# Projections as 64-row halves between the score products of a two-tower attention kernel

## The chip, the cores and the metric

The kernel runs on one core of one Trainium2 chip. The metric is the device time of one execution in microseconds (us); lower is better. The engines are PE (TensorE matmul, with its weight loads shown as PEld), DVE (VectorE), ACT (ScalarE), POOL (GpSimd) and SP (SyncE, which here only issues DMAs).

## What is computed

Two attention blocks share the input x (2048 tokens, 640 features), each with its own weights; each has 32 heads of 20 features. A sigmoid gate mixes the two results.

```python
qkv = (x @ wqkv).reshape(B, S, 3, H, Dh)          # S=2048, H=32, Dh=20, for A and for B
scores = einsum("bhqd,bhkd->bhqk", q, k) * Dh ** -0.5
p = softmax(scores, axis=-1)
o = einsum("bhqk,bhkd->bhqd", p, v)
y = o.transpose(0, 2, 1, 3).reshape(B, S, D) @ wo
out = g * y_A + (1 - g) * y_B                      # g = sigmoid((x * gate_w).sum(-1))
```

## The kernel before

The 64 heads are taken in 16 groups of four. For each group and each block of 512 queries the kernel makes eight steps of 256 keys, 512 steps in all; the number of a step is `G`. PE works in tiles of 64 rows by 32 columns in nearly all of a step: side 0 is rows 0 to 63 of the array, side 1 rows 64 to 127, and what one side does runs beside what the other does. The order of PE's work in a step is written out by hand in the table `STEP` (line 55), by these letters, with the side as the digit:

- `e0`, `e1`: the score product of one head, 128 keys by 512 queries (`scores`, line 704; four matmuls at line 167 in the four column tiles of a side). ACT then takes the exponential of the bank (line 714).
- `m0`, `m1`: a second score product, queries by keys, that only serves to find the maximum of a later step's rows (`max_mm`, line 638; the same line 167). DVE reduces the bank (line 665), or ACT takes a Relu (line 658) and DVE finishes (line 662). A step has eight `e` and about eight `m`, of which one goes to ACT.
- `V0`, `V1`: half of the values product of the step before (`values`, line 724, matmuls at line 730), accumulated in the side's own accumulator `acc0` or `acc1`; four per side and step. One is float32 and two passes long.
- `X`: a turn for one block of the linear layers, by `slot` (line 1229): a part of a chunk of Q/K projection (`project_chunk`), a V projection of 128 tokens (`project_v`) or a part of an output row block (`out_tiles`). Each block is 6 to 15 matmuls of 128 rows by 128 columns in the helper `mms` (line 442), all into one bank, followed by one copy (ACT lines 469, 608, 800, 803, DVE line 806).

Products go to PSUM banks. Two of the eight are the accumulators; six (`bank0` to `bank5`, shown as bank_90 to bank_95) are shared by `e`, `m` and blocks. `take` (line 139) gives a product the bank that by the planner's clock comes free first; `give` returns it with the time at which its reader will be done. The choice is made when the program is built, so on the chip a product waits for just that bank's last reader, and PE takes its instructions in order.

Of a chunk (512 tokens) three or four parts were made, each a block of its own with its own bank and copy (`CUTS`, `APARTS`, `RPARTS`); `behind` decides whether a step has none, one or two blocks. In the last steps, where no maxima are left, `LATE` stands for `STEP`.

Of the kernel before, what the change touches and what calls it, by code (L numbers as in the profile page):

```python
# [19 lines left out]
P = 128  # L20
# [6 lines left out]
GH = 4  # L27
# [11 lines left out]
CUTS = {3: (0, 176, 344, 512), 4: (0, 128, 256, 384, 512), 5: (0, 104, 208, 312, 416, 512), 6: (0, 88, 176, 264, 344, 432, 512)}  # L39
APARTS = {2: 4, 3: 4, 4: 4, 5: 4, 6: 4}  # L40
RPARTS = {1: 4}
# [10 lines left out]
OFINE = (16, 16, 6, 16)  # L52


STEP = ("e1 V0 m1 e1 V0 m1 e0 V1 m0 e0 V1 m0 m1 V0 e1 m1 V0 e1 m0 V1 e0 m0 V1 e0",
        "e1 V0 m1 e1 V0 m1 e0 V1 m0 e0 V1 m0 X m1 V0 e1 m1 V0 e1 m0 V1 e0 m0 V1 e0",
        "e1 V0 m1 e1 V0 m1 e0 V1 m0 e0 V1 m0 X m1 V0 e1 m1 V0 e1 m0 V1 e0 m0 V1 e0 X")
LATE = "e1 V0 e1 V0 e0 V1 e0 V1 X e1 V0 e1 V0 e0 V1 e0 V1"
# [14 lines left out]
def kernel(  # L73
# [80 lines left out]
    def tick_score(j, i):  # L154

        clock["pe"] = max(clock["pe"], rows_free[j], free_at[i])
        rows_free[j] = clock["pe"] + T_SCORE
        clock["done"] = max(clock["done"], clock["pe"] + T_READY)
        return clock["done"]

# [8 lines left out]
    def tick_values(j, ready):  # L169

        clock["pe"] = max(clock["pe"], rows_free[j], ready)
        rows_free[j] = clock["pe"] + T_VALUES
        clock["done"] = max(clock["done"], rows_free[j] + T_READY - T_SCORE)

# [259 lines left out]
    def mms(i, out_ap, pairs, cost):  # L434

        if now[0] >= 0:
            tick_block(len(pairs) * cost * T_SCORE, free_at[i])
        for k, (a, b) in enumerate(pairs):
            if now[0] < 0:
                tick_block(cost * T_SCORE, free_at[i])  # L440
                streamed[0] += cost * T_SCORE
            nc.tensor.matmul(out_ap, a, b, start=(k == 0), stop=(k == len(pairs) - 1))  # L442
            if now[0] < 0:
                yield True

# [5 lines left out]
    def project_chunk(w, hi, lo, ch, parts=None):  # L451
# [9 lines left out]
        if now[0] >= 0:  # L461
            f = work.tile([P, QB], F32, name="fs")
            for k in range(len(parts) - 1):
                if k:
                    yield
                m = slice(parts[k], parts[k + 1])
                i, pt = take()
                yield from mms(i, pt[:, m], pairs(slice(t0 + m.start, t0 + m.stop)), (m.stop - m.start) / QB)
                nc.scalar.activation(f[:, m], pt[:, m], AF.Copy, scale=QKS)  # L469
                give(i, spend("act", 0.25, clock["done"]))  # L470
            nc.gpsimd.tensor_copy(hi, f)  # L471
            nc.gpsimd.tensor_tensor(lo, f, hi, op=OP.subtract)
        else:
            i, pt = take()
            yield from mms(i, pt, pairs(slice(t0, t0 + QB)), 1)
# [42 lines left out]
    def project_r(i, ch):  # L518
        n = slice(ch * QB, (ch + 1) * QB)
        yield from project_chunk(blk["r", i], rk[i][:, 0, n], rk[i][:, 1, n], ch, CUTS[RPARTS.get(i, 3)])  # L520
# [25 lines left out]
    def project_a(g, ch):  # L546
# [4 lines left out]
        yield from project_chunk(blk["a", g], hl[:, 0, n], hl[:, 1, n], ch, CUTS[APARTS.get(g, 3)])  # L551
# [45 lines left out]
    def project_v(gg, j):  # L597

        wh, wl = blk["v", gg]
        w = 161 if gg == 0 else 160  # L600
        for u in range(2):
            if u and now[0] >= 0:
                yield
            n = slice((j + u) * P, (j + u + 1) * P)
            i, pt = take()
            yield from mms(i, pt[:, :w], [(a[:, c, n], b[:, c, :w]) for c in range(NC) for a, b in
                                          ((xh, wh), (xh, wl), (xl, wh))], 0.33)
            nc.scalar.activation(V[gg % 2][:, j + u, :, 0:DH], pt[:, :160].rearrange("p (h d) -> p h d", h=2 * GH),
# [115 lines left out]
    def values(G, kk, side, part):  # L724
# [4 lines left out]
        for h in range(GH):  # L729
# [3 lines left out]
            if side and part:  # L733
                ptiles.pop((G, kk, h))
# [33 lines left out]
    def out_tiles(job, t, state):  # L768
# [15 lines left out]
        cuts = (0, 216, 432, 640) if t >= OFINE[jobs.index(job)] else (0, 320, 640)  # L784

        def products():
            wh, wl = wo_parts[z]
            for k, end in zip(cuts, cuts[1:]):
                if k:
# [4 lines left out]
                yield from mms(i, pt[:, :width], [(o[:p, a, c - c0], w[:p, c, n])  # L794
                                                  for c in range(c0, c1) for p in (P if c < full else 48,)
                                                  for a, w in ((0, wh), (0, wl), (1, wh))], width / QB)
                f = f_o[z][:, t:t + 1]
# [21 lines left out]
        soon(state["due"], len(cuts) - 1, products())  # L819

    def take_acc(g, qb):
# [3 lines left out]
        nc.scalar.activation(total, accs[0], AF.Copy)  # L825
# [4 lines left out]
        nc.vector.tensor_tensor(total, accs[1], total, op=OP.add)  # L830
# [80 lines left out]
    def last_tiles(qb, o):  # L911
# [3 lines left out]
        for t in range(4):  # L915
            c = slice(t * P, (t + 1) * P)
            f = f_o[1][:, 4 * qb + t:4 * qb + t + 1]
            for half in range(2):
# [3 lines left out]
                tick_block(0.4, free_at[i])  # L922
                for k, (a, w) in enumerate(((0, wh), (0, wl), (1, wh))):
                    nc.tensor.matmul(pt[:, :320], o[:, a, c], w[:, n], start=(k == 0), stop=(k == 2))  # L924
# [234 lines left out]
    for g in range(2 * NG):  # L1159
        b = g * step  # L1160
        n = g + 1
        if n < 2 * NG:
            parts = APARTS.get(n, 3)
            fill += [((-8, 15)[g] if g < 2 else b + AFROM, b + ADUE + ADUES * ch if g else 4 + 3 * ch, parts, project_a(n, ch))
# [4 lines left out]
            if i < 4:  # L1169
# [5 lines left out]
                if g % 4 == 2:  # L1175
                    tasks(b + 6, 3, weights_r(i))
                    parts = RPARTS.get(i, 3)
                    fill += [(b + 12, b + 26 + 6 * ch if i == 1 else b + 22 + 4 * ch, parts, project_r(i, ch)) for ch in range(4)]
            gg = g // 2 + 1
            if gg < NG and g % 2 == 0:  # L1180
# [5 lines left out]
                fill += [(max(b + 2, 12), b + 2 * step - 4 + j // 2, 2, project_v(gg, j)) for j in range(0, NT, 2)]  # L1186
# [21 lines left out]
    def out_tasks(G):  # L1208
# [8 lines left out]
        if last and all(4 * last[0][0] + t in summed for t in range(4)):  # L1217
            soon(now[0] + 6, 4, last_tiles(*last.pop(0)))

    def behind(G):  # L1220

        n = sum(f[0] for f in current)
        for f in sorted((f for f in fill if f[0] <= G), key=lambda f: f[1]):
# [133 lines left out]
```

## Time and profile before

| what | value |
|---|---|
| median of 3 runs | 2828.87 us (2828.64 to 2833.61) |
| the profiled execution | 2828.82 us |
| its span, first to last instruction | 2827.0 us |
| busy share PE, PEld, DVE, ACT, POOL | 98%, 56%, 87%, 89%, 25% |
| granted clock of PE, mean | 0.999 |
| first and last exponential begin at | 100.8 and 2807.3 us |

A row of the page's groups names the line, the engine, the operation, what is written and read with the shapes, the count, then the busy time in us and the mean duration of one in ns, and after the second bar the idle time of the engine before these instructions with what ended most of it. A row of the timeline begins with the start in us and the time until the last of the merged instructions ends. The durations of PE's matmuls are modelled, so their starts are read and not their ends.

### The profile page before, as it was taken

What the parts mean: (1) busy time and instruction counts of PE and PEld (TensorE: products, weight loads), DVE (VectorE), ACT (ScalarE), POOL (GpSimd) and SP (SyncE); (2) the same over time, 40 slices, a digit from 0 to 9 for tenths busy, and PEclk for the clock granted to TensorE, in tenths of its full rate; (3) what the DMA queues carried; (4) which work ended last, traced back from release to release, by engine and by line L of the source; (5) the groups of instructions that cost most, each with busy time, mean ns of one, the idle gap of its engine ahead of it and who ended that gap; (6) DMA issues with size and microseconds to landing.
All of it is one profiled execution on the core that took longest, in us unless ns stands there. A gap on an engine that the chain in (4) does not pass through costs nothing.

```text
span 2827.0 us, 163418 instructions
## 1 busy us (share of the span) xinstructions
PE 2784.2 (98%) x72102; PEld 1593.8 (56%) x72102; DVE 2460.6 (87%) x4777; ACT 2530.0 (89%) x5211; POOL 697.8 (25%) x1009
## 2 busy tenths in 40 slices
PE   9999999999999999999999999999999999999998
PEld 4555555555555555665555555555566555555444
DVE  8789898898899989888888898989988888999982
ACT  4999999999999999999999889989999888999887
POOL 6132222222123422212122122223342202101111
PEclk9999999999999999999999999999999999999999
DMA  4021102010120212102021230211201112132112
GB/s 142 17 58 25 33 18 44 9 35 18 24 56 20 66 45 53 36 13 62 21 54 49 68 87 23 69 51 47 66 20 42 36 47 64 34 80 63 46 50 76
DMA packets 175809, 132.05 MB, mean 47 GB/s; under 512 B 103672, under 2 KB 145456, under 8 KB 175096
## 3 DMA queue, kind: packets, MB, share of 16 engines
q1 hardware_dynamic: 172552, 120.31, 16.7%
q8 instruction: 563, 9.22, 1.3%
q0 software_dynamic: 1600, 0.96, 0.2%
q14 instruction: 150, 1.23, 0.1%
q10 hardware_dynamic: 944, 0.33, 0.0%
HBM read 55.53 MB, written 31.86 MB: 31 GB/s over the span
## 4 chain that ended last, share of the span: by engine, by line
PE 85%; ACT 8%; DVE 3%; issue 2%; DMA 1%; POOL 1%; ACTq 0%; SPq 0%; POOLq 0%; DVEq 0%
PE bank L167 43%; PE acc L730 20%; PE bank L442 20%; ACT pt L714 7%; DVE mpart L665 2%; PE bank L164 1%; DMA ws<-in_A_wqkv_dram 0%; PE bank L924 0%; PE acc L442 0%; DMA xs<-in_A_x_dram 0%; DMA kt<-mrow 0%; ACT rl L658 0%; DVE rl L662 0%; DVE y_out L806 0%; ACT ob L825 0%
## 5 line engine op out<-in xcount | busy, mean ns | idle before, releaser
L714 ACT ACTIVATE pt<-bank 128x512 f32<-128x512 f32 x4096 | 2172.5, 633 | 190.2 <-PE bank L167 145.4
L665 DVE TENSOR_REDUCE mpart<-bank 128x1 f32<-128x512 f32 x2944 | 1875.0, 681 | 255.6 <-PE bank L167 166.2
L730 PE MATMUL acc<-pt,v 64*21 64x256 f32 x32768 | 2068.8, 380 | 12.1 <-DVE ob L830 10.5
L167 PE MATMUL bank<-qt,kt 64*32 64x512 f16 x16384 | 1572.2, 380 | 3.4 <-ACT pt L714 0.7
L167 PE MATMUL bank<-kt,qt 60*32 60x512 f16 x13824 | 1364.2, 380 | 2.5 <-ACT pt L714 0.6
L167 PEld LDWEIGHTS <-kt 64*32 64x32 f16 x16384 | 603.5, 91 | 460.2 <-issue 327.4
L167 PEld LDWEIGHTS <-qt 60*32 60x32 f16 x15872 | 553.2, 90 | 413.6 <-issue 223.2
L730 PEld LDWEIGHTS acc<-pt,v 64*21 64x21 f32 x32768 | 686.9, 96 | 134.2 <-DVE ob L830 27.9
L662 DVE CUSTOM_DVE_ANT_0 rl<-bank,rl 128x512 f32<-128x512 f32 x568 | 384.4, 680 | 16.3 <-PE bank L167 10.0
L658 ACT ACTIVATE rl<-bank 128x512 f32<-128x512 f32 x569 | 375.0, 664 | 5.1 <-PE bank L164 4.7
L442 PE MATMUL bank<-xx,wbh 128*128 128x168 f16 (+3 forms) x2450 | 276.8, 234 | 5.1
L442 PE MATMUL bank<-xx,wbl 128*128 128x168 f16 (+3 forms) x1225 | 253.3, 233 | 0.0
L442 PEld LDWEIGHTS <-wbh 128*128 128x128 f16 x2480 | 197.3, 98 | 70.1 <-issue 60.2
L841 POOL TENSOR_TENSOR ot<-ot,sq 128x512 f32<-128x512 f32 x63 | 66.0, 1048 | 609.8 <-DVE sq L838 609.8
L167 PE MATMUL bank<-kd,qt 60*32 60x512 f16 x2048 | 203.9, 380 | 0.0
L471 POOL CAST cq<-fs 128x512 f16<-128x512 f32 x60 | 36.6, 610 | 516.2 <-ACT fs L469 516.2
L442 PE MATMUL bank<-woh,o_in 128*128 128x320 f16 (+3 forms) x700 | 157.4, 289 | 2.5
L442 PEld LDWEIGHTS <-xx 128*128 128x128 f16 x1920 | 133.3, 97 | 41.1 <-issue 37.2
L442 PE MATMUL bank<-wvh,xx 128*128 128x160 f16 (+1 forms) x1250 | 153.3, 234 | 2.4
L442 PE MATMUL bank<-wvl,xx 128*128 128x160 f16 (+1 forms) x625 | 134.4, 232 | 0.0
L442 PEld LDWEIGHTS <-o_in 128*128 128x128 f16 (+1 forms) x1050 | 90.1, 97 | 66.8 <-issue 44.8
L442 PEld LDWEIGHTS <-wbl 128*128 128x128 f16 x1240 | 121.0, 98 | 4.7 <-issue 1.3
(184 smaller groups left out, 1444.0 us busy)
## 6 DMA issues: line engine op xcount, KB each, us to landing
y_scr<-y_out SPq DMA_DIRECT2D x48, 320.0 KB
y_out<-y_scr SPq DMA_DIRECT2D x32, 320.0 KB
kt<-cq SPq DMA_DIRECT2D x120, 80.0 KB
o_scr<-on SPq DMA_DIRECT2D x240, 40.0 KB
o_in<-o_scr SPq DMA_DIRECT2D x64, 96.0 KB
kt<-cq SPq DMA_DIRECT2D x136, 40.0 KB
wstage<-in_B_wqkv_dram SPq DMA_DIRECT2D x13, 400.0 KB
xs<-in_A_x_dram SPq DMA_DIRECT2D x8, 640.0 KB
```

The lines of the kernel that those rows point to most:

```text
L164: nc.tensor.matmul(pt, stationary, moving, start=True, stop=True)
L167: nc.tensor.matmul(pt[c:c + 32], stationary[:, c:c + 32], moving, start=True, stop=True)
L442: nc.tensor.matmul(out_ap, a, b, start=(k == 0), stop=(k == len(pairs) - 1))
L471: nc.gpsimd.tensor_copy(hi, f)
L658: nc.scalar.activation(relus[u, j], pt, AF.Relu)
L662: nc.vector.tensor_tensor_reduce(rl, pt, rl, 1.0, LOW, OP.add, OP.max, m)
L665: nc.vector.tensor_reduce(m, pt, axis=AX.X, op=OP.max)
L714: nc.scalar.activation(pt, et, AF.Exp, scale=factor(g // 4))
L730: nc.tensor.matmul(accs[side][32 * h:32 * h + VW, c], V[(g // 2) % 2][r, kt, (g % 2) * GH + h, :], ptiles[G, kk, h][r, c], start=(kt == 0 ...
L841: nc.gpsimd.tensor_tensor(t3, t3, sq.unsqueeze(2).to_broadcast([P, 16, 32]), op=OP.mult)
```

## The change

Inside the 512 steps the linear layers no longer run as blocks of 128-row matmuls. `mms` hands its list of products to `weave_job`, which cuts each product at row 64 into a half for side 0 and a half for side 1. `halves_of` issues the halves between the scores: each as four matmuls of 64 rows by 32 columns, at the places `x0` and `x1` of the step's order. All halves of a job accumulate into one bank, which is taken when the job begins and held until the copy after its last half. The halves of one side stand in one cluster and those of the other side in a second cluster, so that the two sides do not write the bank at the same time; `recent` sees to it that a bank of a score has come round between the clusters. A place takes one half of 512 columns, or three of the V projection's 160 columns (cost 0.33), or one or two of an output's 320 columns (cost 0.625).

The chunk is made whole: one job of 15 products of 512 columns, three steps of five halves per side, with one copy. The V projection makes two token blocks in one job of 30 products, with one copy of 320 columns. Of all outputs two parts are made. `begin` starts a job at the beginning of a step and picks the order of the step: 0 (no job), `FEW` (five places per side) or `MANY` (six, where that ends the job).

```diff
-STEP = (...
-        "e1 V0 m1 e1 V0 m1 e0 V1 m0 e0 V1 m0 X m1 V0 e1 m1 V0 e1 m0 V1 e0 m0 V1 e0",
...
+FEW, MANY = 5, 6
+STEP = {0: "e1 V1 V1 m1 V0 e1 m1 e0 m0 V1 e0 m0 e0 V0 V0 m1 m0 V1 e0 m0 e1 V0 m1 e1",
+        FEW: "e1 x0 x0 V1 x0 x0 V1 x0 m1 V0 e1 m1 e0 m0 V1 e0 m0 x1 e0 x1 x1 V0 x1 x1 V0 m1 m0 V1 e0 m0 e1 V0 m1 e1",
...
+    def weave_job(i, entries, cost):
+        w = {"bank": i, "cost": cost, "n": 0, "credit": [0.0, 0.0], "q": ([], [])}
+        for a, b, cols in entries:
+            for side in range(2):
+                r = slice(64 * side, min(64 * side + 64, a.shape[0]))
+                if r.start < r.stop:
+                    w["q"][side].append((a[r], b[r], cols))
+        w["all"] = len(w["q"][0]) + len(w["q"][1])
+        recent["side"] = None
+        weave.append(w)
+        while weave:
+            yield
...
+    def halves_of(side, most=1.0):
+        w = weave[0]
+        q = w["q"][side]
+        if not q or recent["side"] == 1 - side and not recent["known"]:
+            return
+        recent.update(side=side, banks=set(), known=False)
+        w["credit"][side] += most
+        while q and w["credit"][side] >= w["cost"] - 1e-6:
+            w["credit"][side] -= w["cost"]
+            a, b, cols = q.pop(0)
+            w["n"] += 1
+            for c in range(0, P, 32):
+                nc.tensor.matmul(banks[w["bank"]][c:c + 32, cols], a[:, c:c + 32], b, start=(w["n"] == 1),
+                                 stop=(w["n"] == w["all"]), skip_group_check=True)
...
-                i, pt = take()
-                yield from mms(i, pt[:, m], pairs(slice(t0 + m.start, t0 + m.stop)), (m.stop - m.start) / QB)
-                nc.scalar.activation(f[:, m], pt[:, m], AF.Copy, scale=QKS)
-                give(i, spend("act", 0.25, clock["done"]))
+            i, pt = take()
+            yield from mms(i, slice(0, QB), pairs(slice(t0, t0 + QB)), 1)
+            nc.scalar.activation(f, banks[i], AF.Copy, scale=QKS)
+            give(i, spend("act", T_EXP, clock["done"]))
...
+        if now[0] >= 0:
+            i, pt = take()
+            yield from weave_job(i, [(a[:, c, slice((j + u) * P, (j + u + 1) * P)], b[:, c, :w], slice(u * w, u * w + w))
+                                     for u in range(2) for c in range(NC) for a, b in ((xh, wh), (xh, wl), (xl, wh))], 0.33)
+            nc.scalar.activation(V[gg % 2][:, j:j + 2, :, 0:DH],
+                                 pt[:, :2 * w].rearrange("p (t h d) -> p t h d", t=2, h=2 * GH), AF.Copy, scale=QKS)
```

How many instructions the built programs hold: the four-matmul score groups and the values products are as many as before (8064 groups, 16384 matmuls). The linear layers inside and before the steps go from 6786 matmuls of 128 rows (lines 442 and 924) to 492 of these and 29208 of 64 rows. ACT's chunk copies go from 240 to 72 and its V copies inside the steps from 112 to 56. SP's queue and POOL's casts hold the same work. Of the 512 steps, 462 now have halves (before, 490 had a block).

Three places of PE's order, all in or at the end of step 210, show the new places. In the rows below, `kt,qt` or `kd,qt` after the bank is an `m`, `qt,kt` an `e`, `acc_88` and `acc_89` are the accumulators of side 0 and side 1, and every product of scores or halves is four rows of which one is shown. First, the middle of step 210 before: an `m0`, the block of 15 matmuls in its bank 93, then `m1`, `V0` and `e1`.

```order
L730 MATMUL acc_89<-pt,v_87 21x256 x4
...
L167 MATMUL bank_94<-kt_83,qt_81 32x512
...
L442 MATMUL bank_93<-xx,wbh 128x168
...
L442 MATMUL bank_93<-xx,wbl 128x168
...
L167 MATMUL bank_90<-kt_83,qt_81 32x512
...
L730 MATMUL acc_88<-pt,v_87 21x256 x4
...
L167 MATMUL bank_91<-qt_80,kt_82 32x512
```

This block is gone. Second, the beginning of step 210 in the changed program, from its first `e1` (bank 93) to its first `m1` (bank 91): the job's bank is 95, and after the first `V1` come two more halves, the second `V1` and a fifth half, whose rows read like those shown.

```order
L162 MATMUL bank_93<-qt_80,kt_82 32x512
...
L498 MATMUL bank_95<-xx,wbl 32x512
...
L498 MATMUL bank_95<-xx,wbh 32x512
L795 MATMUL acc_89<-pt,v_87 21x256 x4
...
L162 MATMUL bank_91<-kt_83,qt_81 32x512
```

Between the first `e1` and the first `m1` there now stand a cluster on side 0 and two values products on side 1, where one `V0` stood. Third, what follows this `m1` in the changed program, up to the `e0` within the second cluster; the `kd,qt` is the `m0` that ACT reads.

```order
L795 MATMUL acc_88<-pt,v_87 21x256 x4
...
L162 MATMUL bank_92<-qt_80,kt_82 32x512
...
L162 MATMUL bank_90<-kt_83,qt_81 32x512
...
L162 MATMUL bank_94<-qt_80,kt_82 32x512
...
L162 MATMUL bank_93<-kd_85,qt_81 32x512
...
L795 MATMUL acc_89<-pt,v_87 21x256 x4
...
L162 MATMUL bank_91<-qt_80,kt_82 32x512
...
L162 MATMUL bank_92<-kt_83,qt_81 32x512
...
L498 MATMUL bank_95<-xx,wbl 32x512
...
L162 MATMUL bank_94<-qt_80,kt_82 32x512
```

With the `m1` ahead of these rows, eight score products now follow one another with two values products among them, and they use five banks, since bank 95 is the job's: the sixth takes the first's bank (91), the seventh the second's (92), the eighth the fourth's (94). After the second cluster, which ends with two `V0`, the order goes on in the same way with `m1` (90), `m0` (93), `e0` (92), `m0` (91), `e1` (94), `m1` (90), `e1` (92) and, as the first of step 211, `e1` (93).

More of the change, by code (lines that the diff above doesn't have):

```diff
@@ L432, in weights_r, with mms @@
         return load, split
-    def mms(i, out_ap, pairs, cost):
+    weave = []
+    def weave_job(i, entries, cost):
[10 more added lines that the diff above has]
+            yield
+    def mms(i, n, pairs, cost):
+        if 0 <= now[0] < STEPS:
+            yield from weave_job(i, [(a, b, n) for a, b in pairs], cost)
+            return
         if now[0] >= 0:
@@ L1185 @@
                 at(max(b - 1, 10), split)
[L1186 removed]
+                fill += [(max(b + 2, 12), b + 2 * step - 14 + j, 20, project_v(gg, j)) for j in range(0, NT, 2)]
     early = weights_v(NG - 1)
@@ L1288 @@
             product()
-            slot(G)
+            for side in (0, 1):
+                fence()
+                begin(G)
+                for _ in range(4):
+                    slot(G, side)
         some = next_maxima(G, 4)
-        blocks = 0 if not current and not any(f[0] <= G for f in fill) else 2 if behind(G) else 1
+        order = (STEP if maxima or some else LATE[G % 2])[begin(G)]
         count = {}
-        for what in (STEP[blocks] if maxima or some else LATE + " X" * (blocks == 2)).split():
+        for what in order.split():
             k = count[what] = count.get(what, 0) + 1
```

149 lines of the change are left out of this document (91 added, 58 removed).

## Prediction

> **What bounds the kernel now.** I read the page's busy shares and its chain first, then the groups, and last the timeline of one step, engine by engine. The page:
>
> ```profile
> PE 2784.2 (98%) x72102; PEld 1593.8 (56%) x72102; DVE 2460.6 (87%) x4777; ACT 2530.0 (89%) x5211; POOL 697.8 (25%) x1009
> ...
> PE bank L167 43%; PE acc L730 20%; PE bank L442 20%; ACT pt L714 7%; DVE mpart L665 2%; PE bank L164 1%; DMA ws<-in_A_wqkv_dram 0%; PE bank L924 0%; PE acc L442 0%; DMA xs<-in_A_x_dram 0%; DMA kt<-mrow 0%; ACT rl L658 0%; DVE rl L662 0%; DVE y_out L806 0%; ACT ob L825 0%
> ...
> L714 ACT ACTIVATE pt<-bank 128x512 f32<-128x512 f32 x4096 | 2172.5, 633 | 190.2 <-PE bank L167 145.4
> L665 DVE TENSOR_REDUCE mpart<-bank 128x1 f32<-128x512 f32 x2944 | 1875.0, 681 | 255.6 <-PE bank L167 166.2
> ...
> L167 PE MATMUL bank<-qt,kt 64*32 64x512 f16 x16384 | 1572.2, 380 | 3.4 <-ACT pt L714 0.7
> ```
>
> The chain lies on PE for 85%, ACT and DVE are busy for nearly nine tenths, and where these two idle they wait for PE's scores. None of the three is full. What ties them shows only in one step. These are PE's rows from one block to the next (starts are what counts):
>
> ```profile
> 1001.18 0.32 PE L442 MATMUL bank<-xx,wbh 128*128 128x168 f16 x2
> ...
> 1002.21 0.24 PE L442 MATMUL bank<-xx,wbl 128*128 128x168 f16 x1
> 1002.38 0.40 PE L167 MATMUL bank<-kt,qt 60*32 60x512 f16 x4
> 1002.39 0.41 PE L730 MATMUL acc<-pt,v 64*21 64x256 f32 x4
> 1002.60 0.39 PE L167 MATMUL bank<-qt,kt 64*32 64x512 f16 x4
> ...
> 1002.82 0.39 PE L167 MATMUL bank<-kt,qt 60*32 60x512 f16 x4
> ...
> 1003.92 0.78 PE L167 MATMUL bank<-qt,kt 64*32 64x512 f16 x8
> 1004.32 0.41 PE L730 MATMUL acc<-pt,v 64*21 64x256 f32 x4
> ...
> 1004.80 0.40 PE L167 MATMUL bank<-qt,kt 64*32 64x512 f16 x4
> ...
> 1005.29 0.40 PE L167 MATMUL bank<-qt,kt 64*32 64x512 f16 x4
> ...
> 1005.78 0.40 PE L167 MATMUL bank<-qt,kt 64*32 64x512 f16 x4
> ...
> 1006.04 0.37 PE L167 MATMUL bank<-kt,qt 60*32 60x512 f16 x1
> ...
> 1006.37 0.33 PE L442 MATMUL bank<-xx,wbh 128*128 128x176 f16 x2
> ```
>
> After the block a score product begins every 0.22 us (1002.38, 1002.60, 1002.82): that is what one product takes of a side, and a values product, two passes, takes two such slots, 0.43. From 1004.80 on the pairs come 0.49 apart (1004.80, 1005.29, 1005.78): PE waits. For what, ACT's and DVE's rows tell:
>
> ```profile
> 1002.48 0.31 ACT L469 ACTIVATE fs<-bank 128x168 f32<-128x168 f32 x1
> 1003.17 3.54 ACT L714 ACTIVATE pt<-bank 128x512 f32<-128x512 f32 x7 [0.38 <-PE bank L167]
> ```
>
> ```profile
> 1002.89 1.29 DVE L665 TENSOR_REDUCE mpart<-bank 128x1 f32<-128x512 f32 x2 [0.85 <-PE bank L167]
> ```
>
> An `e` that begins at 1002.60 is read from 1003.17: 0.57 later. An `m` of 1002.38 is read from 1002.89: 0.51 later. Seven exponentials take 3.54, one lasts 0.633, so they follow at (3.54-0.633)/6 = 0.485; two reductions take 1.29 and one 0.681, so 0.61. The third exponential thus ends at 3.17+2x0.485+0.633 = 4.77 (I leave out the thousand), and the product of 4.80 begins; the fourth ends at 5.26, and that of 5.29 begins; the fifth at 5.74, and that of 5.78 begins. In the program's order these are the users of the same banks, and the hand-over takes 0.03 to 0.04. So PE's products wait for a bank, and **a bank costs 0.57+0.633+0.04 = 1.24 us for an `e`, 0.51+0.681+0.04 = 1.23 for an `m`, plus the reader's queue.** Six banks and this turnaround set the burst of 16 products; then comes the block, in which ACT and DVE run dry (0.38 and 0.85).
>
> I check this as a rule: every product starts at the latest of its side's slot, the product ahead of it in the order, and the release of its bank. From `m1` at 0 it gives 0, 0.22, 0.44, 0.65, 0.87, 1.08, 1.30, 1.52 (PE's pace), then by releases 1.94, 2.16, 2.42, 2.64, 2.90, 3.12, 3.37, 3.64 and the block at 3.95. The rows say 4.32-2.38 = 1.94 for the `V0` right behind the ninth, 2.42 and 2.91 for the eleventh and thirteenth, and 3.99 for the block. The rule holds within 1% here. All steps:
>
> ```profile
> L714 ACT ACTIVATE pt<-bank x4096: 590/632/1006, 100.8 to 2807.3; 128x512 f32<-128x512 f32 x196
> ```
>
> (2807.3-100.8)/512 = 5.29 us, against 6.37-1.18 = 5.19 in this one, so some 0.1 us per step is other work in the readers' queues that the rule doesn't have.
>
> **The change, part by part.**
>
> *The drains around blocks.* The last matmul of the block begins at 1002.21, matmuls there follow at (1002.21-1001.18)/14 = 0.074, and the next product begins at 1002.38: 0.10 lost. Ahead of the block at 1006.37 the last score began at 1006.04 and had 0.22 to stream: 0.11 lost. Together 0.2 us for each of 490 blocks, 98 us of PE's time that goes. PE's own need hardly falls, though: in a step with 5+5 halves a side has 8 slots of scores, 4 values products and 5 halves, 8x0.217+4x0.433+5x0.217 = 4.55 us, and before it had 3.47 and a block of 1.1 with its drains, 4.77.
>
> *The copies.* Rows of ACT's groups by shape: V copies, chunk copies in three sizes, and a copy of 320 columns:
>
> ```profile
> L608 ACT ACTIVATE v<-bank 128x160 f32<-128x160 f32 x125 | 38.5, 308 | 13.1 <-PE bank L442 12.8
> ...
> L469 ACT ACTIVATE fs<-bank 128x128 f32<-128x128 f32 x96 | 31.7, 330 | 3.3 <-PE bank L442 1.2
> L469 ACT ACTIVATE fs<-bank 128x168 f32<-128x168 f32 x96 | 30.7, 320 | 11.8 <-PE bank L442 11.6
> L800 ACT ACTIVATE y_out<-bank,f_o 128x320 f32<-128x320 f32 x32 | 16.9, 527 | 9.2 <-PE bank L442 7.5
> L469 ACT ACTIVATE fs<-bank 128x176 f32<-128x176 f32 x48 | 15.3, 318 | 9.3 <-PE bank L442 6.0 <-issue 1.9
> ```
>
> 240 chunk copies cost 77.7 us of ACT and become 72 of the size of an exponential, 72x0.633 = 46; 112 V copies at 0.308 = 34 become 56 at 0.527 = 30. ACT loses some 36 us of work. Off the path: the copies stand where ACT waits for scores (the 1002.48 row lies ahead of its 0.38 of idling), so I take 0; on the path it would be -36.
>
> *The order and the banks: the large term.* A job keeps its bank from its first half to its copy, three steps for a chunk, so scores have five banks, where before a block held one for about 1.1 us and its copy. And the step now has two stretches without a score instead of one. I apply the same rule to step 210, whose banks the order shows, from its first `m1` at 0, the queues empty. First burst: `e1` 0.22, `m1` 0.44, `e0` 0.44, `m0` 0.66 are at PE's pace. The sixth (`e0`, bank 91) waits for the first `m1`: 1.23. The seventh (bank 92) waits for the `e1`: 0.22+1.24 = 1.46. The eighth (`e0`, bank 94) waits for the `e0` of 0.44, which stands second in ACT's queue: 0.22+0.57+0.485+0.633+0.04 = 1.95. Then come the other four halves of the second cluster, on side 1, 0.217 each, which hold back `m1`: 2.82. Second burst: `m0` 3.03, `e0` 3.25, `m0` and `e1` 3.47; `m1` in bank 90 waits for the `m1` of 2.82: 4.05; `e1` in bank 92 for the `e0` of 3.25: 4.49; the next step's `e1` for its side, 4.71 (its bank, the `m0`'s of 3.03, is free at 4.66). Then on side 1 that `e1` and two `V1`, 0.217+2x0.433 = 1.08, ahead of the next `m1`: **5.79 us**, against 3.95+15x0.074+0.10 = 5.16 by the same rule before. PE waits 0.36+0.27+0.36+0.22 = 1.21 for banks (without them it would be 4.58), and in each of the two gaps ACT and DVE idle: ACT needs 9x0.485 = 4.37 of 5.79. Behind a waiting score stand the halves and values products of both sides, since PE takes its instructions in order, so the clusters can't fill the wait.
>
> Where the planner always gave the bank that comes free first, the eighth would start at 1.84 and the step take 5.68; that is the lower end. At the upper end the 0.1 us of other work falls into each burst and delays more than itself: 6.05. I take 5.79+0.1 = 5.89, the other work of the average step before. For the 50 steps without halves the rule gives 5.1 with six banks (the two values products between the bursts stay), and the last 14, without maxima, stay as they are: 5.0 on average.
>
> *Issue.* The halves bring 22,900 more pairs of weight load and matmul. The four matmuls of a product take 0.40 from the first's start to the last's end (the row of 1002.38) where one alone takes 0.380, so they start within 0.02, and a values product on the other side starts 0.01 after them; I take issue as 0, with a rival for the other case.
>
> *Sum.* Before 512x5.29 = 2706. After 462x5.89+50x5.0 = 2971. That is +265 on the profiled execution's 2828.8 us, which is the median of the runs shown (2828.87) within 0.1: **3094 us**. The lower end, 462x5.68+250 = 2874, gives 2997; the upper, 462x6.05+250 = 3045, gives 3168.
>
> **The rivals.**
>
> *Drains alone (faster).* If scores rarely wait for a bank, the gain is PE's drains: 2829-98 = 2731. The mechanism: halves run beside `V1` and `V0`, so nothing stops while they stream, and readers are fed in two smaller portions. It decides once a step stays under (2706-250)/462 = 5.32 us, that is if the waits for banks come to under 5.32-4.58-0.1 = 0.64 us in a step instead of 1.21. For it speaks that PE is busy 98%; against it that the same rule hit the step before to 1% with a bank more. The Trainium skill, TensorEngine Tiling (Array Packing), Key Properties, says that a change of tiling mode drains the engine; the trace agrees, with 0.2 us around a block, and by that rule alone the change gains these 98 us. I give it 0.11.
>
> *Copies or nothing.* The bursts' waits are as long as the drains saved, and the step stays at 5.29: 2829, or with the copies' 36 us on the path 2793. 0.04.
>
> *Issue-bound V steps (slower still).* 112 steps would carry 15+15 halves of 160 columns: 32+32 matmuls of scores, 64 passes of values, 120 of halves, 248 pairs. The closest that the step shown has them is a score group and a pass of values, eight pairs, in 0.22 us: 27 ns. At that price 248 pairs take 6.7 us instead of 5.89: +91, 3185. Against it: there PE streams, and issue isn't what is short. The Trainium skill, TensorEngine Tiling (Array Packing), Instruction Overhead, has about 60 cycles for each matmul; no run here shows one by itself. By it, an estimate at the 2.4 GHz of its page TensorE: Matmul & The Clock Gate, 216 matmul instructions at 25 ns make 5.4 us, under the 5.89, and the rival falls. 0.05.
>
> **How the numbers follow.** Forecast 0.80, drains alone 0.11, nothing or copies 0.04, issue 0.05. A measurement of this kernel can tell about 0.2% from no change. Faster: 0.11 and half of the third case, 0.13; same 0.02; slower 0.85. The forecast's own range is 2997 to 3168; to hold 8 in 10 it goes down to 2900 (a step of 5.47, with two thirds of the waits worked out) and up to 3190, past the issue case.
>
> **What would show it.** Right: steps near 5.9 us by the exponentials' starts; ACT's share falls to 80 to 84%, its idle time ahead of the exponentials rises from 190 to over 400 us; in the timeline the sixth product after a cluster starts 1.2 to 1.3 us after the first. Wrong: scores that follow at 0.22 through both bursts, ACT at 92% or more, a step under 5.3. If V steps alone are long, it is issue; if the starts of halves lie over 0.22 apart beside a `V1`, the two sides disturb one another, which no row of before shows.

## The result, and the profile after

| | before | after |
|---|---|---|
| median | 2828.76 us (2828.44 to 2833.61, 4 runs) | 3232.09 us (3221.65 to 3234.53, 4 runs) |
| ratio | | 1.1414, interval 1.1386 to 1.1442 |
| profiled execution, span | 2828.82, 2827.0 us | 3233.22, 3231.1 us |

The change costs 403 us. The direction was forecast, the size was not: 3094 us, with a range up to 3190. These are the lines of the page after that answer to those of before: busy shares, the packets of the instruction queue, the chain, and the groups of the exponentials and of the scores' weight loads.

```profile
PE 3040.5 (94%) x95016; PEld 1767.8 (55%) x95016; DVE 2516.1 (78%) x4763; ACT 2599.2 (80%) x4991; POOL 704.6 (22%) x1013
...
q8 instruction: 742, 12.16, 1.6%
...
PE 76%; DVE 9%; ACT 6%; issue 5%; DMA 1%; POOL 1%; SPq 0%; ACTq 0%; DVEq 0%; POOLq 0%
...
L779 ACT ACTIVATE pt<-bank 128x512 f32<-128x512 f32 x4096 | 2241.9, 611 | 532.3 <-PE bank L162 456.9
...
L162 PEld LDWEIGHTS <-kt 64*32 64x32 f16 x16384 | 611.2, 91 | 667.3 <-issue 525.1
```

Of the same page before, two lines that the prediction did not read:

```profile
q8 instruction: 563, 9.22, 1.3%
...
L167 PEld LDWEIGHTS <-kt 64*32 64x32 f16 x16384 | 603.5, 91 | 460.2 <-issue 327.4
```

ACT and DVE are each 9 points less busy, and ACT idles for PE's scores: 532 us ahead of the exponentials where it was 190. PE issues 190,032 instructions where it issued 144,204 (loads and matmuls of the first line), and the instruction queue brings 742 packets instead of 563. 742x256 = 189,952 and 563x256 = 144,128: the queue brings PE's program, 256 instructions in a packet. The scores' loads stand idle for 667 us where it was 460, and 198 of the 207 us more are put down to "issue", that is to nothing that the profile shows.

Eight exponentials make a step. The times between their starts, sorted by the shape of the halves in the step (counted through the trace, steps 16 to 495, mixed steps left out), give: 203 steps with chunk halves 5.81 us, 117 with output halves 5.95, 49 without halves 5.12, and **110 with V halves 7.30**. The forecast had 5.89 for all with halves and 5.0 for those without. So the hand rule hit three kinds of steps within 2.5% and missed the fourth by 1.41, which over 112 steps is 158 us, somewhat more than the 138 that the total lies above the forecast.

First the part that came as forecast. PE's rows of one step with chunk halves, from the first half of its first cluster to that of the next step's:

```profile
1151.74 0.40 PE L498 MATMUL bank<-xx,wbh 64*32 64x512 f16 x4
...
1152.80 0.40 PE L162 MATMUL bank<-kt,qt 60*32 60x512 f16 x4
...
1153.02 0.40 PE L162 MATMUL bank<-qt,kt 64*32 64x512 f16 x3
...
1154.06 0.40 PE L162 MATMUL bank<-qt,kt 64*32 64x512 f16 x4
...
1157.40 0.40 PE L498 MATMUL bank<-xx,wbl 64*32 64x512 f16 x4
```

After the cluster the first `m1` begins at 1152.80, four products follow at PE's pace, and the sixth, which takes the first one's bank, begins at 1154.06: 1.26 later, where the rule had 1.23. The step is 5.66 long, the rule's was 5.79.

Now a step with V halves. PE's rows around one stall, and for the ten microseconds around it the instruction queue: the second view cuts its window, 1002 to 1012, in 40 slices of 0.25 us and gives each the rate of all DMA.

```profile
1004.29 0.39 PE L795 MATMUL acc<-pt,v 64*21 64x256 f32 x2
1005.33 0.40 PE L795 MATMUL acc<-pt,v 64*21 64x256 f32 x3 [0.65 <-issue]
...
1007.79 0.61 PE L795 MATMUL acc<-pt,v 64*21 64x256 f32 x5
1008.75 0.39 PE L795 MATMUL acc<-pt,v 64*21 64x256 f32 x1 [0.35 <-issue]
```

```profile
GB/s 0 0 66 0 0 0 0 0 0 0 0 0 0 0 0 0 0 66 0 0 0 0 0 0 0 0 0 0 0 0 0 66 0 0 0 0 0 0 0 0
...
q8 instruction: 3, 0.05, 2.1%
```

Twice PE stops among the matmuls of one values product, where there is no bank and no reader to wait for, and goes on with the rest 0.7 to 1 us later. The only transfers in these 10 us are three packets of instructions, at 1002.5, 1006.25 and 1009.75. Counted through the whole trace, PE starts nothing for over 0.45 us at 551 places, and 203 of them lie in 32 of the 256 positions that an instruction's number can have modulo 256; evenly spread it would be 69. Before, there are 111 such places, and 17 of them in these 32 positions, where 14 would be even. The restarts follow the packets, too: of the 21 such places in the ten V steps from 992 to 1067, 15 end 2.2 to 2.8 us after a packet's transfer has begun. So the **theory: in V steps PE runs out of instructions, which come 256 at a time** (the expectations call it the fetch theory). The rivals: short products (160 columns may not hide their weight loads), the V job itself (its operands, its bank, its copy), and the clusters' order.

### The profile page after: what moved, and what is told of

It is laid out like the page before. It is cut to its first block, busy times and chain, and to the rows that moved or that the text cites. A ratio compares the mean times of both kernels' runs of the same rounds, so it can differ in the third digit from the quotient of the medians.

```text
span 3231.1 us, 209868 instructions
## 1 busy us (share of the span) xinstructions
PE 3040.5 (94%) x95016; PEld 1767.8 (55%) x95016; DVE 2516.1 (78%) x4763; ACT 2599.2 (80%) x4991; POOL 704.6 (22%) x1013
## 3 DMA queue, kind: packets, MB, share of 16 engines
q14 instruction: 154, 1.26, 0.1%
## 4 chain that ended last, share of the span: by engine, by line
PE 76%; DVE 9%; ACT 6%; issue 5%; DMA 1%; POOL 1%; SPq 0%; ACTq 0%; DVEq 0%; POOLq 0%
PE bank L162 34%; PE acc L795 31%; PE bank L498 9%; DVE mpart L730 6%; ACT pt L779 6%; DVE rl L727 2%; PE bank L472 1%; PE bank L159 1%; DVE mpart L727 1%; DMA ws<-in_A_wqkv_dram 0%; ACT y_out L864 0%; DVE mneg L737 0%; PE acc L472 0%; DMA xs<-in_A_x_dram 0%; DMA kt<-mrow 0%
## 5 line engine op out<-in xcount | busy, mean ns | idle before, releaser
L795 PEld LDWEIGHTS acc<-pt,v 64*21 64x21 f32 x32768 | 973.1, 96 | 282.3 <-issue 39.6
L498 PE MATMUL bank<-xx,wbh 64*32 64x512 f16 x5760 | 475.9, 380 | 0.9 <-issue 0.9
L498 PE MATMUL bank<-wvh,xx 64*32 64x160 f16 x8960 | 333.6, 232 | 17.3 <-issue 16.3
L498 PE MATMUL bank<-woh,o_in 64*32 64x320 f16 (+1 forms) x4624 | 284.3, 298 | 0.0
L498 PE MATMUL bank<-xx,wbl 64*32 64x512 f16 x2880 | 282.1, 380 | 0.0
L498 PE MATMUL bank<-wvl,xx 64*32 64x160 f16 x4480 | 266.3, 229 | 11.2 <-issue 11.0
L498 PEld LDWEIGHTS <-xx 64*32 64x32 f16 x13440 | 232.4, 91 | 55.2 <-issue 52.9
L498 PE MATMUL bank<-wol,o_in 64*32 64x320 f16 (+1 forms) x2312 | 180.9, 298 | 0.1
L498 PEld LDWEIGHTS <-o_in 64*32 64x32 f16 x6936 | 161.4, 92 | 12.3 <-issue 1.3
L498 PEld LDWEIGHTS <-wbh 64*32 64x32 f16 x5760 | 137.7, 91 | 5.6 <-issue 3.2
```

The source lines that it names most:

```text
L498: nc.tensor.matmul(banks[w["bank"]][c:c + 32, cols], a[:, c:c + 32], b, start=(w["n"] == 1), stop=(w["n"] == w["all"]), skip_group_check=True)
L795: nc.tensor.matmul(accs[side][32 * h:32 * h + VW, c], V[(g // 2) % 2][r, kt, (g % 2) * GH + h, :], ptiles[G, kk, h][r, c], start=(kt == 0 ...
```

## The experiments

Each run was timed against the kernel before on the same chip. In the expectations (up to the run of the rate) the count of PE's instructions in a step is too low: it has 16 matmuls of values products in a step, and the trace has 64 (32,768 in 512 steps, each with its load). With them a chunk step has 336 (not 240), a nine-product output step 400, a V step 496 (not 400), and the cases meant as 220, 280 and 320 have 316, 376 and 416. The rows below show it. They compare the same stretch of the program, steps 148 to 157, which in the kernel after all have V halves; in the kernel before the like ten steps are 152 to 161. A row has the window, its length, then busy time and count of PE's matmuls, PE's loads, DVE, ACT and POOL, the granted clock, and DMA. Before, and after with a second stretch of 12 chunk steps:

```profile
891.73:945.73 54.00, 53.34 (x1446) 32.21 (x1431) 47.29 (x90) 48.87 (x104) 21.53 (x19) 1.00 0.11 27
```

```profile
992.11:1066.95 74.84, 64.91 (x2478) 43.11 (x2465) 47.62 (x89) 50.36 (x97) 20.97 (x25) 1.00 0.13 33
1112.19:1181.55 69.36, 66.74 (x2000) 34.04 (x1988) 59.83 (x114) 59.46 (x115) 16.19 (x23) 1.00 0.19 44
```

That is 5.40 us and 288 instructions a step before; after, 7.48 and 494 with V halves, 5.78 and 332 with chunk halves.

### V as blocks again

```diff
 def project_v(gg, j):
...
-        if now[0] >= 0:
+        if False:
             i, pt = take()
             yield from weave_job(i, [...], 0.33)
...
         for u in range(2):
+            if u and now[0] >= 0:
+                yield
...
-                                          ((xh, wh), (xh, wl), (xl, wh))], 0.33)
+                                          ((xh, wh), (xh, wl), (xl, wh))], 0.33, True)
```

> The V projections go back into whole blocks of 128 rows, in the order of the steps that the kernel before had for a block; chunks and outputs stay in halves. V steps took 7.30 us on average in the changed kernel (110 of them), 5.34 as blocks before. If the excess of the V steps is all that the forecast missed: V steps near 5.4, the others as they are (chunk 5.81, output 5.95), total 3232-110x1.9 = 3023 us. If something beside them was missed too (chunk and output steps long for a reason that the V steps cause, for example by what they leave in the queues), the others get shorter as well and the total falls under 2990. If V steps are long whatever the form of the products, the total stays over 3150.

3026.71 us (3026.13 to 3028.94). The stretch:

```profile
922.45:976.59 54.14, 52.55 (x1438) 32.26 (x1429) 46.27 (x89) 48.53 (x103) 17.63 (x23) 1.00 0.12 33
```

5.41 a step, with the other kinds as they were (chunk steps 5.82 and output steps 5.95 on average). The V projection as halves costs 205 us, and nothing else in the kernel hangs on it. A step with a block also has the old order and its six banks again, so this run alone doesn't say what in the halves costs so much.

### Half the instructions, the same columns

```diff
-[(a[:, c, ...], b[:, c, :w], slice(u * w, u * w + w)) for u in range(2) ...], 0.33)
+[(a[:, c, ...], b[:, c, :w].unsqueeze(1).to_broadcast([P, 2, w]), slice(0, 2 * w)) for u in range(1) ...], 0.66)
```

> The V job multiplies only the first of its two token blocks, 15 products of 320 columns (the weights read twice) where there were 30 of 160; the second block's values are copies of the first's, so half of the V projection is left out. Columns streamed stay the same, PE's instructions in a V step fall from some 400 to some 280. Fetch theory (PE runs out of instructions, which come 256 at a time): V steps 5.8 to 6.0, total 3232-110x1.4 = 3078. Short-product theory (160 columns are too short to hide four weight loads): the same, 3078. Theory that it is the V job's operands, bank or copy: V steps stay near 7.3, total 3232.

3072.39 us (3072.17 to 3076.53).

```profile
937.69:995.18 57.49, 55.70 (x1887) 35.63 (x1873) 47.66 (x89) 49.75 (x97) 19.44 (x25) 1.00 0.13 32
```

376 instructions, 5.75 us: the excess is gone with job, bank, copy and clusters unchanged. The theory of the V job falls, and so does the clusters' as far as V steps go; short products remain.

### As short, but fewer in a step

```diff
-                 for a, b in ((xh, wh), (xh, wl), (xl, wh))], 0.33)
+                 for a, b in ((xh, wh), (xh, wl), (xl, wh))], 0.5 if gg < 4 else 0.33)
```

> The V jobs of the first three groups (24 of 56) give two halves at each place instead of three, so such a job takes three steps of 10+10 halves instead of two of 15+15, each half as before: 320 of PE's instructions in a step instead of 400. Fetch theory: these 72 steps take 5.5 to 6.0 (output steps with some 304 instructions take 5.95), total 3232-(48x7.30+24x5.12-72x5.9) = 3184. Short-product theory: each half costs (7.30-5.85)/30 = 0.048 too much, so 20 of them make 5.85+0.97 = 6.8 per step, total about 3250.

3196.05 us (3192.11 to 3204.15). A stretch of 18 steps, nearly all with 10+10 halves:

```profile
969.66:1079.89 110.23, 104.18 (x3743) 65.40 (x3730) 85.70 (x159) 88.87 (x172) 40.37 (x45) 1.00 0.16 37
```

415 instructions, 6.12 us; all 72 such steps of the trace, sorted by PE's own order, take 6.13 on average. That is a little over the 5.5 to 6.0 of the fetch theory, but at 0.048 for each half 6.8 was due. Short products fall: it is how many there are in a step.

### One wide matmul for four narrow ones

```diff
-            for c in range(0, P, 32):
-                nc.tensor.matmul(banks[...][c:c + 32, cols], a[:, c:c + 32], b, ...)
+            m = P if w["cost"] == 0.33 else 32
+            for c in range(0, P, m):
+                nc.tensor.matmul(banks[...][c:c + m, cols], a[:, c:c + m], b, ...)
```

> Each V half goes as one matmul of 64 rows by 128 columns instead of four of 64x32: one weight load and one matmul instead of four and four, 220 of PE's instructions in a V step instead of 400, with the same columns streamed. Fetch theory, with the tile's width free of charge: V steps 5.8 to 6.0, total 3078. If a change of the tile's width drains as a block did (0.2 us, ten places in a step, some of them joined): V steps 5.9+10x0.2 = 7.9, total near 3300. If a 64x128 load doesn't hide behind 160 columns: in between, 6.5 to 7, total 3150 to 3200.

3450.75 us (3448.77 to 3451.53).

```profile
1061.41:1151.34 89.93, 88.48 (x1599) 42.65 (x1600) 47.56 (x89) 49.94 (x98) 20.93 (x25) 1.00 0.11 27
```

320 instructions and 8.99 us, more than any of the three cases had; nearest is the rival in which a change of the tile's width drains like a block (7.9). PE's rows between two values runs there:

```profile
1061.66 0.63 PE L796 MATMUL acc<-pt,v 64*21 64x256 f32 x8
1062.22 0.24 PE L499 MATMUL bank<-wvh,xx 64*128 64x160 f16 x1
...
1062.59 0.23 PE L499 MATMUL bank<-wvh,xx 64*128 64x160 f16 x1
1062.74 0.63 PE L796 MATMUL acc<-pt,v 64*21 64x256 f32 x8
```

Two passes of values take 0.43, and the first half begins 0.56 after them (1062.22-1061.66); six halves at 0.074 take 0.44, and the values begin 0.52 after the first of them (1062.74-1062.22). So some 0.2 us is lost around a cluster, as around a block. And nothing of the other side starts while these halves go, where narrow halves ran beside values products; that this makes up the rest, over the 7.9, is argued and not tried. This run tells nothing of the price of an instruction; it shows that instructions can't be saved in this way.

### More instructions where there were few

```diff
-    def project_chunk(w, hi, lo, ch):
+    def project_chunk(w, hi, lo, ch, cuts=(0, 256, 512)):
...
-            yield from mms(i, slice(0, QB), pairs(slice(t0, t0 + QB)), 1)
+            yield from weave_job(i, [...], 1 / (len(cuts) - 1))
...
-        yield from project_chunk(blk["r", i], rk[i][:, 0, n], rk[i][:, 1, n], ch)
+        yield from project_chunk(blk["r", i], rk[i][:, 0, n], rk[i][:, 1, n], ch, (0, 176, 344, 512))
```

> Chunk halves are cut along their columns, with the same columns in all: those of the 60 chunks of A in two of 256 (320 of PE's instructions in a step instead of 240), those of the 12 chunks of R in three of 176 and 168 (400, as in a V step). Fetch theory, with its threshold: A's 180 steps stay at 5.8 to 6.0, R's 36 steps go to 7.1 to 7.4, total 3232+36x1.45+180x0.1 = 3300 us. A price for each further pair ((7.30-5.81)/80 = 19 ns, whatever their number): A's steps +0.75, R's +1.5, total 3232+135+54 = 3421. If it is the V job's own operands and not the count: nothing changes, 3232.

A and R are the two kinds of chunk that the kernel makes (`project_a`, `project_r`). 3338.8 us (3335.78 to 3344.68), nearer to the threshold's 3300 than to 3421. Twelve steps of A, then eight of R:

```profile
1153.84:1226.70 72.86, 68.90 (x2452) 43.44 (x2441) 60.24 (x114) 59.99 (x114) 16.14 (x23) 1.00 0.18 42
```

```profile
1391.95:1446.44 54.49, 51.26 (x1993) 33.50 (x1980) 38.73 (x71) 40.35 (x76) 12.75 (x17) 1.00 0.04 8
```

408 instructions take 6.07, 497 take 6.81 here; through the whole trace A's steps take 6.17 on average and R's 7.09. Chunk halves become nearly as slow as V halves once they are as many, so it isn't V. A sharp threshold is not what is seen: A's steps, expected at 5.8 to 6.0, already pay. A pace for every instruction, which the next run measures, gives them 416x14.4 = 6.0.

### The rate by itself

```diff
     run(last_tiles(NQ - 1, end_o))
+    for k in range(960):
+        j = k % 2
+        r = slice(64 * j, 64 * j + 64)
+        for c in range(0, P, 32):
+            nc.tensor.matmul(banks[j][c:c + 32, :160], QT[0][r, 0, (k // 2) % 16 * P + c:(k // 2) % 16 * P + c + 32], KT[0][r, 0, :160],
+                             start=True, stop=True)
```

> The kernel before, and behind its last matmul 960 products in the form of the V halves (four tiles of 64x32, 160 columns, sides in turn, two banks of their own, weights that change): 3840 pairs of weight load and matmul that nothing waits for and that wait for nothing, 7680 instructions, 30 packets of 256. Counting the passes of the values products fully, a V step of the changed kernel has 248 pairs, 496 instructions, not 400 as the runs ahead had it, a chunk step 336, an output step with nine products 400. Fetch theory: packets came at best 3.46 us apart (5 in 100 were closer), 13.5 ns an instruction; 7680 of them take 104 us, in bursts with a stall once in 256, total near 2829+104 = 2930. If issue is steady at the 10 ns seen between stalls, 77 us and no stalls. If only the columns count, 480x0.067 = 32 us.

2935.59 us (2933.48 to 2937.32), 106.6 above the kernel before. The group's row, three bursts of the matmuls in the timeline, the queue over this time, and the granted clock in it:

```profile
L1333 PE MATMUL bank<-kt,qt x3840: 226/337/338, 2821.7 to 2932.3; 64*32 64x160 f16 x192
```

```profile
2852.61 2.33 PE L1333 MATMUL bank<-kt,qt 64*32 64x160 f16 x128 [1.69 <-issue]
2856.36 2.34 PE L1333 MATMUL bank<-kt,qt 64*32 64x160 f16 x128 [1.42 <-issue]
2859.84 2.33 PE L1333 MATMUL bank<-kt,qt 64*32 64x160 f16 x128 [1.14 <-issue]
```

```profile
q8 instruction: 30, 0.49, 2.0%
```

```profile
2825.00:2930.00 105.00, 65.20 (x3584) 58.53 (x3584) 0.00 (x0) 0.00 (x0) 0.00 (x0) 0.51 0.02 5
```

With nothing to wait for, PE issues 128 loads and 128 matmuls, stops, and begins the next 128 and 128 3.75 us after the last (2856.36-2852.61), then 3.48 (2859.84-2856.36), once for each of 30 packets; from the stop to the next start it is 1.1 to 1.7 us in these rows. Counted through these products, from the first stop of over 1 us on there are exactly 256 instructions from each stop to the next, and each restart comes 2.3 to 2.9 us after a packet's transfer has begun. 7680 instructions take 110.6 us, **14.4 ns each**. The clock fell to 0.51 here. But the V stretch, at 1.00, has 74.84 us for 4943 instructions, 15.1 ns, and R's chunk steps 54.49 for 3973, 13.7: the same pace at twice the clock.

### Without the halves' work, with five banks and with six

```diff
-            for c in range(0, P, 32):
-                nc.tensor.matmul(banks[w["bank"]][c:c + 32, cols], ...)
```

The run with six banks also has

```diff
         weave.append(w)
+        held.discard(i)
         while weave:
             yield
+        held.add(i)
```

> All matmuls of the halves are left out (chunks, V and outputs are not computed); the order, the copies and the bank that each job holds for its steps stay. Bank theory: the rule gives 5.63 without the halves where it gives 5.69 with them, so steps take 5.6 to 5.75 of whatever kind, total 3232-110x1.6-350x0.15 = 3003 us. If PE's own work sets the step (4.55 us a side with halves, 3.47 without), steps fall below 5, total under 2650.

> As the kernel without halves' matmuls, and a job's bank is left to the scores until its copy: six banks instead of five, the same work, the same order. Bank theory: the rule gives 5.03 with six banks and 5.63 with five; 462 steps by 0.6 less, total 3003-277 = 2726 us. If banks don't bound the step, no difference from the run with five.

3023.28 us (3022.1 to 3024.0) with five, 2832.13 (2829.53 to 2833.93) with six. PE's line of the page of each, and its exponentials:

```profile
PE 2910.9 (96%) x65808; PEld 1562.3 (52%) x65808; DVE 2509.1 (83%) x4763; ACT 2591.0 (86%) x4991; POOL 703.0 (23%) x1013
...
L776 ACT ACTIVATE pt<-bank x4096: 592/598/1326, 101.0 to 2985.0; 128x512 f32<-128x512 f32 x196
```

```profile
PE 2749.6 (97%) x65808; PEld 1541.2 (55%) x65808; DVE 2476.9 (88%) x4763; ACT 2512.9 (89%) x4991; POOL 703.8 (25%) x1013
...
L778 ACT ACTIVATE pt<-bank x4096: 592/618/1379, 101.2 to 2791.4; 128x512 f32<-128x512 f32 x196
```

All 29,208 matmuls of halves are gone and the step is (2985.0-101.0)/512 = 5.63 (5.69 without the short last ones), where the rule gives 5.63 for the order without them; the halves' work doesn't set it. (PE still reads 96% busy, with a third fewer instructions: that share is no sign of a full PE.) One bank more brings 5.25. The direction is the rule's, the size is 191 us instead of the 277 expected; why the sixth bank is worth less here was not tried.

### The kernel before with five banks

```diff
-    held.add(NB - 1)
+    held.update((0, NB - 1))
```

> The kernel before with one of its six banks never used in the steps. By the rule a step with a block goes from 5.19 to 5.57, one without from 4.36 to 4.66: 480x0.38+31x0.3 = +192, total 3021 us. If banks don't bound the kernel before, 2829.

3012.27 us (3011.15 to 3012.68), ratio 1.0635 (1.0617 to 1.0652): +180 on the 2832.33 of the kernel before on the same chip, for 192 expected. So the rule's price of a bank holds in the old order too.

### Evenly mixed orders

```diff
-FEW: "e1 x0 x0 V1 x0 x0 V1 x0 m1 V0 e1 m1 e0 m0 V1 e0 m0 x1 e0 x1 x1 V0 x1 x1 V0 m1 m0 V1 e0 m0 e1 V0 m1 e1"
+FEW: "V1 V0 e1 V0 m1 m1 e0 x1 x1 m0 x1 V0 x1 x1 m0 e0 V1 V0 e1 m0 V1 e0 m1 x0 e1 x0 V1 e0 m1 x0 x0 x0 e1 m0"
...
```

> V as blocks, and the steps with halves get an order in which scores, values products and halves are mixed evenly: no stretch with over three halves in a row, both sides' scores alternating, side 1's halves over five scores, side 0's over five later ones. Same instructions, same five banks. Bank and order theory: the rule gives 4.77 for a step with 5+5 halves (5.69 in the clustered order) and 4.93 with 6+6; measured steps lay 0.1 above the rule, so chunk steps 4.9, output steps 5.0, total 3027-350x0.85 = 2730 us. If five banks hold a step above 5.6 in any order: 3000 or more. If instructions come too slowly for 240 to 300 in 4.9 us (256 in 3.7 us at the fastest seen): output steps 5.3 to 5.5, total near 2800.

> As the run with the evenly mixed order and V blocks, and the steps without halves too get a mixed order (rule: 4.32 to 4.50 with six banks, 5.03 in the order of the change): 43 steps by 0.5, total 2730-22 = 2708 us.

> The changed kernel with the evenly mixed order in the steps with halves; V stays in halves, three at a place. Fetch theory: 400 instructions take 6.6 to 7.3 in any order, so V steps keep nearly all of their time while chunk steps fall to 4.9 and output steps to 5.0: total 3232-350x0.85-110x0.3 = 2900 us. If the V steps' excess came with the clusters: V steps fall to 5 as well, total 2680.

2876.99 us (2874.87 to 2879.82), 2867.98 (2863.8 to 2874.89) and 3088.12 (3087.39 to 3089.44). Of the first, two and then five neighbouring chunk steps, 200 and 201, 203 to 207; of the third, the V stretch:

```profile
1168.01:1179.56 11.55, 10.94 (x348) 5.98 (x343) 10.36 (x20) 10.10 (x21) 5.09 (x5) 1.00 0.29 66
1184.91:1209.15 24.24, 24.20 (x848) 16.38 (x847) 22.71 (x41) 23.88 (x48) 10.26 (x11) 1.00 0.05 11
```

```profile
956.56:1028.62 72.06, 57.94 (x2480) 41.91 (x2476) 48.46 (x89) 50.71 (x97) 20.59 (x24) 1.00 0.13 34
```

The order is worth 150 us with the same work and the same five banks, half of the 297 expected. The five steps take 4.85, what the rule says; but they hold 339 instructions each, which at 14.4 ns are 4.88, so these rows don't tell the banks' limit from the instructions'. Steps 200 and 201 take 5.78: there a block of queries ends, ACT and DVE read the accumulators into `ob`, and the order's first `V1` and `V0` wait for that, as the group of the values products' loads says:

```profile
L801 PEld LDWEIGHTS acc<-pt,v 64*21 64x21 f32 x32768 | 788.0, 96 | 242.0 <-DVE ob L900 41.3 <-ACT ob L895 18.6 <-issue 16.6
```

The expectation had no such term; it is 41.3+18.6 = 60 us of the 147 by which 2730 was missed. Counted through the trace, chunk steps take 5.8 in the first two places of a block of queries and 5.2 in the other six, where 4.9 was expected. Output steps take 5.42: the banks had 5.0, and the case in which instructions come too slowly had 5.3 to 5.5. So part of the rest is probably the instructions' pace again; no run here separates it. The mixed order in the steps without halves brought 9 us of 22. The third run missed its 2900 by 188, since chunk and output steps fell as little as in the first; its difference to the first, 211 us, is that of V in the old order (205), and its V steps keep 7.21, as the theory has it. None of the three beats the kernel before; the nearest is at 1.0138 (1.0118 to 1.0158) of it.

## Why the prediction was wrong, and where it was right

- **Order and banks, the large term: right.** Chunk steps 5.81 and output steps 5.95 for 5.89, the sixth product 1.26 after the first for 1.23, ACT at 80% and 532 us idle ahead of the exponentials as "What would show it" had them. The bank was priced on its own (180 us for 192), and the halves' work shown to be nearly hidden (5.69 without them, 5.81 with). Off the two orders for which it was worked out the rule was too hopeful: the sixth bank brought 191 us of 277 and the mixed order 150 of 297. With V steps at 5.89 the total would have been 3232-158 = 3074, 20 below the forecast. In the output steps two limits lie together: by 14.4 ns 400 instructions are 5.76; which of the two ends last there was not separated, so their 5.95 doesn't speak for the rule alone.
- **Issue, "I take issue as 0": the step that failed.** In V steps it was 1.41 us, some 158 us in all: 496 instructions at 14.4 to 15.1 ns set the step, 7.30 on average, and not the banks' 5.89. The row that I read, four matmuls of a product starting within 0.02, is the pace within a burst. It says nothing of the pace over 256 instructions, and the view that does, the packets of the instruction queue, I did not read. The trace before held a warning: in its steps no two packets come closer than 3.49 us, and 496 instructions in 5.89 us need one every 5.89x256/496 = 3.04.
- **The rival "issue-bound V steps" was the case, and had 0.05.** Its price, 27 ns for a pair, comes close to what the rate run gives (110.6/3840 = 28.8), and its 6.7 us for 248 pairs to the 7.2 to 7.5 measured; I had taken it from a place where PE streams columns, and so disbelieved it; that the figure comes out near the pace of the instructions is luck. The sign named for it, V steps alone long, is what came. The Trainium skill, TensorEngine Tiling (Array Packing), Instruction Overhead, was used to let it fall, with about 60 cycles for each of 216 matmuls. The values products' second passes are matmuls of their own in the trace: 248, which at the same 25 ns are an estimate of 6.2, over the 5.89. So that figure of the Trainium skill, counted rightly, spoke for the rival, though it is still short of the 7.30 measured.
- **Drains, copies.** The copies were taken as 0 and the 98 us of drains as no gain of their own. Neither was tried apart, so that both lie off the path stays an argument.
- **Steps without halves**, 5.1 by the rule (5.0 with the last 14), 5.12 measured ahead of those: right.
- **A stall that no step of mine had.** In step 387 DVE waits once for POOL, and POOL for PE:

```profile
2474.10 0.71 DVE L908 STREAM_TRANSPOSE ob<-ot 128x512 f32<-128x512 f32 x1 [11.74 <-POOL ot L905]
```

```profile
2463.33 0.85 POOL L383 CAST wvh<-wstage 128x800 f16<-128x800 f32 x1 [47.80 <-PE bank L498]
```

POOL wants to write the next group's V weights while the last V job still reads the old ones, and all that is queued behind it on POOL is late, 11.7 us for DVE's transposition and with it PE. It is read from the trace, not tried, and small.

## What to carry to other kernels

Count the instructions of a step beside its columns: cutting products into tiles of a quarter or an eighth multiplies loads and matmuls, and here PE is bound by them from some 400 in 5.8 us on (14.4 ns each, in lots of 256), in V steps, in chunk steps and in products that wait for nothing. A busy share of PE does not tell this; the number of packets in the instruction queue does, and so do idle gaps "for issue" in the middle of a product. A bank that is held over steps is paid for in the readers' turnaround (180 us for one of six here), and the same work in an even order gave back 150 us.

## What the runs showed of the hardware

- Instructions came in packets of 256, some 3.5 to 4 us apart where PE used them up, and PE stood still for up to 2.5 us when it had. What sets these 3.5 us (the transfer itself, or when it is asked for) no run here tells. The Trainium skill, Runtime: NRT & Kernel Launch, Instruction fetch mechanics, has the blocks of 256, as the trace does, but calls fetching hidden because instructions are dispatched more slowly than blocks arrive. Here it is the other way round: in the rows of the rate run PE has issued a block 1.1 to 1.7 us before the next one begins.
- With V halves as tiles of 64x128 between tiles of 64x32 a step took 8.99 us, against 5.75 with tiles of 64x32 and as many columns (the run with half the instructions): 3.2 us more for some ten such places, with the rows on the same sides throughout. Some 0.2 us at each place is read from PE's rows.
- In the run of the rate the granted clock was 0.51 over 105 us, while PE stopped for 1.1 to 1.7 us at a time in the rows shown and for 2.5 at most; in the V stretch it was 1.00.
